# GpSimd issues none of the last output tiles' stores, with another order of the work

## The chip, the cores and the metric

The kernel runs on one core of one Trainium2 chip. The core has a matrix engine (TensorE, PE in the profile, with its weight loads as PEld), VectorE (DVE), ScalarE (ACT), GpSimd (POOL) and SyncE (SP), which run side by side and wait for each other on semaphores. Transfers between device memory and on-chip memory are DMAs; in this kernel SP, ACT and GpSimd issue them. The metric is the time of one execution on the device in microseconds (us). 13 runs of the kernel before gave a median of 248.54 us, from 246.45 to 251.24.

## The reference

Attention through 32 packed queries per head, and then a feed-forward layer with a squared ReLU:

```python
def _attn_ref(q, k, v, p):            # q, k, v: (8, 8, 576, 64), p: (8, 8, 32, 64)
    p_packed = sm_attn(p, k, v)       # softmax(p k^T / 8) v
    out = sm_attn(q, p_packed, p_packed)
    ...
x = attn_out.transpose(0, 2, 1, 3).reshape(4608, 512)
h = x @ w_in                          # (512, 2048)
r = np.maximum(h, 0.0)
out = (r * r) @ w_out                 # (2048, 512)
```

## The kernel before

The work is cut by batch (8 batches of 576 tokens) for the attention and the first matrix product, and by output tiles of 128 tokens (36 tiles, 0 to 35) for the second product. The kernel doesn't issue its work in the order of the source. It builds steps, each a chain of pieces, and every piece has one or more alternatives: an engine, an estimate in us and a function that issues the instructions. `Plan.run` (L62) then issues all 1,696 pieces in an order written out by hand in the string `ORDER` (L77): decoded, it is one 16-bit number for each piece, in which the low 12 bits are the place in the order and the upper 4 choose the alternative, so the engine. Every engine runs its own instructions strictly in the order in which they were issued; waits between engines follow from the data and the buffers. The estimates in the code have no part in the order once the string is there.

The names of the steps that the text uses, with batch b, tile t:

- `Lk.b.q`, `Lq.b.q`, `Lv.b.0.i` (L661 to L677): loads of k, q and v, issued on GpSimd, which casts float32 to bfloat16 on the way. v comes in four parts (i = 0 to 3). `LWI`, `LWO`: the two weights. Eight buffers hold k and q, two hold v.
- `Cv.b.q` (L686): a copy of v into one tile, `v_b` (L251), on DVE. It needs all four parts of v, and the buffer of v is free for batch b + 2 after it.
- `Tk`, `Tq` (L691): transposes of k and q on DVE, and for batches 4 to 7 of q as DMA transposes on SP (L281).
- `S1`, `PV`, `XT`, `M`, `S2`, `N`: the attention, with q's side folded into w_in by `M`. `X.b` on GpSimd lays out p. `XT.b` takes the packed result out of PSUM (`pp`, `pq`, `rD`), and `S2.b` needs that.
- `R.b.fb` (L790): four matmuls of the first product for one of 16 blocks of 128 columns, and the ReLU out of PSUM on ACT (L499) or DVE (L501), through two PSUM tiles `ps_h`. `F1.b.fb` (L798): the square of two such blocks into `gT`, mostly on DVE (L510). Four buffers `r` lie between, each of two blocks.
- `F2.t.fb` (L850): the second product for one tile. Tiles 7 to 34 are done in groups of four (L896) with seven half-size products instead of eight, `F2.t.n.kk` with n = 1 to 7; `WS.t.n.h` (L882) are the sums of g that they need, on DVE (L606). Results leave the PSUM banks `ps_o` on ACT (L170) or DVE (L172, L633) into one of three output buffers `o_sb`. The last tile, 35, is done in two halves of 256 columns (L861), the first evicted by DVE, the second by ACT.
- `ST...` (L827): the stores of an output tile, in pieces of two DMAs of 32 rows each (64 KB; 32 KB for a half of tile 35). Each piece may go to SP; to GpSimd from tile 8 on, and to ACT from tile 31 on. A group's tiles t and t + 1 are stored after its product 6 (`ST.t.6`), t + 2 and t + 3 after product 7 (`ST.t.7`).

`FILL` (L75) names steps in front of whose matmuls TensorE runs extra ones on a tile of zeros (`keep_clock`, L190), 97 in all, in the first 27 us.

In the order before, the last 24 DMAs of the stores (tiles 31 to 35) are 10 on GpSimd, 6 on SP and 8 on ACT.

Of the kernel before, what the change touches and what calls it, by code (L numbers as in the profile page):

```python
# [76 lines left out]
ORDER = (  # L77
    'c-jrt17j5m7y!`EVd3s-)mm;DtJSit)t23smR2phwrsm)+qP}nw)x(#I0rx=2_%A~kP{3NLssyC<d6rFfg6H>At7V}FQkRy;0t~b0;wS*l!E+F'
    '0IESQ2!cvb1}Z``C<$dD9I8Vd=mQO)IgEx*&<z$sD`*chpfc2iE>Ig9!VstcRiQ16fU$5G2E$0$3QZsqCPGgb0IOjEEQM>Z9M-`tm;jUEEKGyh'
    'a0xcUPIv@2;2tEvy>JNLzzH}9-{B5C1t&g+*N_HZzz4{Tf<9OQ^I#$DitpeH1fv^MV_p0Tf1wzb#!A==t6(i0h&8c3j>kaEjV*C8uEmp>5wl@q'  # L80
    'oPi5)54ORMxEkl<ay)=f@eL9+$F?{ZH{x!*hVStQ`cX~_p_cRtKcX*9!CAN&SK<~thei%6Lf`NYrls_hjj9n-BFamXXcn!cxwM!zQYy+smFW>a'
    '!w)!?rqB|q%}sd#XQ3c!K-IY}_vQf3#QC`ix8k8ZgXYsZy2RJ{F_+=0+?p$KICtjJG=XMPDo)2a_zK_Q_gsieazif0<+wR#<Gfs%GjdKY$_NS$'
    'AV>iIkPb39(mMhn3uJQ?0w=h@11F&<6oXgr9!B6;{EEM^EA^*j?B=PwjO$5PNdYM#4Wx1eIL<>NOo=-%DV?QBoEdUJFSr6Vurpr5JNOS%6R`3k'
    'KE;(KO7cQ^Xbdet(Tg*2116*jRFSGuZ>mXkr~_@GU38ST(>}UD-}oOVl0S@+N|K6O0>vd>36kuP8}dOBC<uk21eAtyPzA!Eh9eYi!hN_4Pv9B6'
    'gpcqUe!?#YVKM~Y_Sgmc-~{ZCgK#>o!cDl<_Yj`K`@RqG2|mZq_zr&|l2Bqw?krB_ojGU~ZK5@Fg7(r8I!EW}GF_otbc3EyPwvb8c@z)gaXgu)'
    '@C=^C3wXY39%qvrl1qw9J}DxlrL2^f3hpqeDOKG^<+vP^Q*v5v%L92VPvyD$wY-xz?pjb6>N)zsFo=aUupTx#w!jY9?O=3ZDh$PT*Z?2n3*VQR'
    'm5Nb5I!>pYr|BBqcHW^rJdlU*7@o+}IlJVS+)_+RNg4MEIVYFpt~_)<l6KlzJ9_%)AkP4;4^5#FL_lk32OXg$w1E!L8KNK>x<U+ehe0qLdO&aJ'
    '4{?wIb72+?!6H}<Yhz(7i(%LVe<F~QliZYn3Xq5VDLa*<<+PgC(^lF+7wH3Sqy6-VUeQZ>L!ame{U+vm{F9JVZ~<P*>v#ok;qAPikMTC%!$<fQ'
    '*OB_tR9Z?K=_iAwqjZ*$vQ$cH8Lg^~w5hh&?%F~lHA?$xUl`~Z3ZoojV7y}-OoAye(=i?9z<gK?OJD_ThkbAmj=~W*1!v$gT!5=^9UeL!z*~3@'
    'pB&w=H}=53z5{SL4#8144yWNnoQLta6qn&TT#vhOJMPDWcoYxgaXgLZ@d94PD|j7m;BBlzH7JzAsV+69Ce*?iNm0~}qNxjYqwds)`q3a7OmWU('  # L90
    'G=fIbIGRY)XgbZId9;8Q(o!N$$O$+JCuJ9VIHfB!r{@fug|l-I=i`E0m`ibKuE15e7Kd?tZp@L~lB2jCcjQhS!~6K4>oA|-lYEBH@&&%kH~1z$'
    ';79y|U-BD%$DjEN|Kh)_Vv<;rh_5)sPy8jVJB_55*3w?ONH^&ry`_)zcMp^y5-Y=Ggp6~Kmx(e}X38v?C-Y^IES6=mLRQNfSua~;hwPNS@>V{$'
    '-^&;Gcljm1<)5&ciYC@1np_>~Qjezc_-lZs(~O#3b7@`;)&g2s!?mu~)&@F4N9!mZ>zSaFb&^iknL0=3>T+GCt9703)-Af%b4<_a1-<OKsyFnO'
    '-qrj1NFVD{eW9;BQz0H!!8W)Ex8Vnv?_ivSD{vnk!LxW1A7UeFPd#ZMjiRZvh*nTq4&*#sf@^RKj^<u`o}ch5{>mZ_$tYQ+mrRx!GFKMLI@u#f'
    'B$4{6pC_~C)M8pro9jHC@7d%zqSy6~KG%;r4;H~nSPQ#g5A25n@DCDVI!uq5FgxbOd{_Wy!CY7d8(<S0gX3@-{s3Z8EQL|n38OIv`{6hE4T&)c'
    'CdK6Fi!StFR?LC<u?$wkde{&n&<|6fKL%i0%!%c&Dptoj*a(|qGi-s8*c!WI5EjJZSRPwp2kePnil?=-fi}}_I!Mpx8+GS?JeXs71W(|Nyp>Z*'
    'PRT35Qb=k`b7>{p<fNRD3vyNN$q)G>q^e0ZpBB{WI$THURGp;@b*XOEQ~FcE5}VunExl#6oL1e!Z6uDtIk*tF;a)t3C-4kj#H)A<@8Ugtjc+lt'
    '^Amo-@AwxJkPjuHWaOe0l#&7{4W*-u6iBt4c_=>xQ$Z?BMX3apqS92B%26e%PGMA=8d7s=MiJDCI#Oqfp<dLNVrc*kp`kRK#?W}0OtWbj?W8?)'
    'fDX}NIz}hy3|*&7bd_$>UAjm2=>a{Y7xb8((sO!EZ|NPqr;qfDKGPTaO5f=Z{iS~-oS2Ohu@5`h%l@2(Gjn-YR?f}A9Kyx9ELY@e+}2fx8*npj'
    '!yUK_cjF#Bmg9IB59g6Qn#c1rp2>@OHqYU?9M21R2`}fByxO&j*YH|i&l`9XZ{{7mi+A#F-pdF05Fh2^e44NFIljo(_%=V}r~I1V@(0%^{>i_Y'  # L100
    'C8798GVw@iNg)A}PBKU)$t+nUkCc!CQcyyquoRV&QcfyL4XGqmq?%NhP^l&1Qdb(e8%RTGEKQ`Dw2%milupuC+DQkAmKf<SJ*BS<l>stH;$*mt'
    'k_j?Nrpqe#Y>AfzvP724N?9u#<dAHY-Lg;i%K<qoXXU)yl#6mnuE;gHE;r<s+>!h8M4rhDc`2{tqkNLj@=d<VPx&kVqpt}xq57y-lc`hPnnF`*'
    'YE7eQHN9rgOd6;;G`Hs05G|smJVmv*meA5#R?BN;t)jKGn%2-z4bysBUmI#;ZKcgLLR)HUZKG|qgLcxM8m(QltHx+I?V-K2xAxQiI#37e5RKJ1'
    '9je20qK?sVI$o#fG@YTdHC|Wh0$rqwb&0OfRk}vk>SoV2-KBeUpYGR#dRUL@2|c4{^}JrxD|$_D>TP|X_w=DY(P#QnU+WuvtMB!le$Y?)S-<F4'
    '{ifgbm;TV-`bYojKm9+0#-=7_mcSBPBJ;5%mei74GIN-(In8ArOKGVrz*1WpOJ^A@qXk+v%Wk<Whvl{)%V+s5*a})9D`JJMs1>skR?<pYX)9yp'
    'tgMx{3Rcl7S!JtYRjr0qvrwyPwJgkPTOF%w^{t*Yu!h#i8e0=<YR#;LHMa<hw3gP&T3dVTV4ba_b+TydVlmdux?2zHX}zqU^|t{w$Oc=i4YxQO'
    'Y9nl<jk3`;#>U$On`o14icPg?Hr-~}EGvN}u`-5ZERM!uI2Ge?GS0>&I20G*8r+GwC^r?NGE|S6QhjPmt*H%lq8^l-9qh-sT)wU%9LhDhy{i#N'
    'xVrLPe(t)*&-lLUBY$TQa{q88kmNF2#<-`sr^r~DBO7It>~e3H&F+JeMYC!)Pmm{%7Sak@QEPfCdFptY=z86t+jXPofS%MHdfIcyv(s~2FR9lG'
    'n4hJ!6yD;N$+B1;%k0hT4Y4-XHn6KV%G!B{Sa0iN1HF9%hXqcyu{O>-(>u>*+Z>x47;papcrZuK'
)  # L110
# [918 lines left out]
```

## Time and profile before

| what | value |
|---|---|
| median of 13 runs | 248.54 us (246.45 to 251.24) |
| the profiled execution: its time, its span | 249.91 us, 248.0 us |
| mean granted clock of TensorE | 0.981 of full speed |
| GpSimd: store DMAs x58, mean of one | 28.7 us, 502 ns |
| ReLU on ACT (L499) x97, on DVE (L501) x15, mean of one | 650 ns, 755 ns |
| square on DVE (L510) x60, mean of one | 752 ns |
| 64 KB stores, median from issue to landing: SP, GpSimd, ACT | 2.8, 2.3, 3.5 us |
| chain that ended last, share of PE / DMA / DVE / POOL | 69% / 13% / 6% / 3% |

The page gives times of one profiled execution; it took 1.37 us more than the median of the runs, and its span, from the first to the last instruction, is 1.9 us shorter than its time. In the rows by slices the span is cut in 40 equal parts of 6.2 us, and a digit is the busy share in tenths. PEclk is the clock that TensorE was granted. A wait names the engine and line that waited, what released it, the total, how often and the longest.

### The profile page before, as it was taken

How to read it: one execution, taken by the hardware profiler on the slowest of the kernel's cores; microseconds unless marked ns; L12 is line 12 of the kernel's file. 1: busy time of each engine (PE TensorE's matmuls, PEld its weight loads, DVE VectorE, ACT ScalarE, POOL GpSimd, SP SyncE). 2: the span in 40 equal slices, each digit the busy share in tenths (PEclk: the TensorE clock that was granted, in tenths of full speed). 3: DMA queues.
4: the chain of work that ended last, by engine and by line, in shares of the span. 5: the costliest groups of instructions: out<-in, count | busy, mean ns of one | idle time of the engine just before them, and what ended most of it. 6: DMA issues, size and time to landing. Idle time of an engine off the chain costs nothing.

```text
span 248.0 us, 6006 instructions
## 1 busy us (share of the span) xinstructions
PE 227.6 (92%) x2407; PEld 174.1 (70%) x2417; DVE 180.9 (73%) x315; ACT 158.8 (64%) x265; POOL 88.8 (36%) x177
## 2 busy tenths in 40 slices
PE   8587989999999889999969999999999999999960
PEld 6465556467656756888648878887888788888850
DVE  3666779689997588988768699798887698765400
ACT  3337468799978759788848776878576857412110
POOL 8585468517573012083711400141007005104070
PEclk9799999999999999999999999999999999999995
DMA  6999999999999995079950980032005104206070
GB/s 215 180 206 203 198 200 207 204 228 213 232 204 216 169 188 95 3 130 179 228 95 15 158 189 3 6 102 68 1 3 146 27 0 108 65 3 169 0 213 1
DMA packets 35708, 31.43 MB, mean 127 GB/s; under 512 B 15232, under 2 KB 28160, under 8 KB 35680
## 3 DMA queue, kind: packets, MB, share of 16 engines
q0 software_dynamic: 21328, 21.67, 51.3%
q1 hardware_dynamic: 13824, 8.33, 15.3%
q10 hardware_dynamic: 528, 1.05, 1.3%
q8 instruction: 19, 0.31, 0.5%
q14 instruction: 9, 0.07, 0.1%
HBM read 37.22 MB, written 9.44 MB: 188 GB/s over the span
## 4 chain that ended last, share of the span: by engine, by line
PE 69%; DMA 13%; DVE 6%; POOL 3%; ACT 2%; issue 2%; POOLq 0%; SPq 0%; DVEq 0%
PE ps_o L620 30%; PE ps_h L470 17%; DMA k_b<-in_k_dram 4%; PE ps_o L561 4%; DMA q_b<-in_q_dram 3%; PE ps_h L480 3%; DMA v_r<-in_v_dram 3%; PE ps_m L383 3%; DMA k_f<-in_k_dram 3%; PE ps_a L561 3%; PE ps_a L296 2%; PE ps_pp L331 2%; PE ps_s L192 1%; PE ps_s L444 1%; POOL out_dram L541 1%
## 5 line engine op out<-in xcount | busy, mean ns | idle before, releaser
L499 ACT ACTIVATE r<-ps_h 128x576 bf16<-128x576 f32 x97 | 62.5, 650 | 21.4 <-PE ps_h L470 18.8
L470 PE MATMUL ps_h<-a,M 128*128 128x288 bf16 x448 | 71.7, 286 | 1.7 <-DVE r L501 1.5
L541 POOL DMA_DIRECT2D out_dram<-o_sb x58 | 28.7, 502 | 101.9 <-DVE o_sb L633 91.9
L510 DVE TENSOR_TENSOR gT<-r 128x1152 bf16<-128x1152 bf16 x60 | 44.8, 752 | 13.4 <-ACT r L499 10.1
L470 PEld LDWEIGHTS <-M 128*128 128x128 bf16 x448 | 43.7, 98 | 12.5 <-issue 2.1
L620 PEld LDWEIGHTS <-wS 128*128 128x128 bf16 x448 | 42.6, 98 | 9.3 <-issue 3.2
L620 PE MATMUL ps_o<-wT,wS 128*128 128x256 bf16 x336 | 41.7, 273 | 0.4 <-DVE wS L606 0.4
L620 PEld LDWEIGHTS <-gT 128*128 128x128 bf16 x336 | 32.7, 98 | 5.7 <-issue 0.2
L620 PE MATMUL ps_o<-w_out_b,gT 128*128 128x256 bf16 x224 | 32.5, 273 | 0.0
L170 ACT COPY o_sb<-ps_o 128x512 f32<-128x512 f32 (+1 forms) x24 | 13.8, 575 | 24.4 <-PE ps_o L620 21.1
L247 POOL DMA_DIRECT2D v_r<-in_v_dram x32 | 19.3, 609 | 24.3 <-DVE r L501 9.4
L170 ACT CAST M<-ps_m 128x1024 bf16<-128x1024 f32 (+1 forms) x26 | 23.5, 930 | 2.7 <-PE ps_m L383 2.5
L561 PE MATMUL ps_o<-w_out_b,gT 128*128 128x512 bf16 x72 | 21.2, 380 | 0.5
L606 DVE TENSOR_TENSOR wS<-gT 128x1024 bf16<-128x1024 bf16 (+1 forms) x32 | 19.1, 617 | 0.2
L633 DVE TENSOR_TENSOR o_sb<-ps_o,o_sb 128x512 f32<-128x512 f32 x21 | 14.4, 684 | 5.1 <-issue 2.9
L561 PEld LDWEIGHTS <-gT 128*128 128x128 bf16 x112 | 10.1, 98 | 10.3 <-issue 2.0
L620 PE MATMUL ps_o<-wT,gT 128*128 128x256 bf16 x112 | 16.3, 273 | 0.0
L620 PE MATMUL ps_o<-w_out_b,wS 128*128 128x256 bf16 x112 | 15.8, 273 | 0.0
L501 DVE TENSOR_SCALAR r<-ps_h 128x576 bf16<-128x576 f32 x15 | 11.2, 755 | 5.9 <-PE ps_h L470 5.9
L192 PEld LDWEIGHTS <-idle_b 128*128 128x128 bf16 x97 | 11.1, 118 | 6.3 <-issue 3.8
L458 DVE SCALAR_TENSOR_TENSOR a<-e,rD,ls 128x576 bf16<-128x576 bf16 (+1 forms) x18 | 13.0, 743 | 2.8 <-ACT ls L452 2.7
L438 ACT ACTIVATE e<-ps_s,rD 128x576 bf16<-128x576 f32 (+1 forms) x18 | 11.4, 683 | 4.8 <-PE ps_s L430 2.8
(84 smaller groups left out, 317.8 us busy)
## 6 DMA issues: line engine op xcount, KB each, us to landing
out_dram<-o_sb SPq DMA_DIRECT2D x80, 64.0 KB, 2.8
k_b<-in_k_dram POOLq DMA_DIRECT2D x14, 288.0 KB, 9.6
q_b<-in_q_dram POOLq DMA_DIRECT2D x14, 288.0 KB, 8.4
out_dram<-o_sb POOLq DMA_DIRECT2D x54, 64.0 KB, 2.3
v_r<-in_v_dram POOLq DMA_DIRECT2D x16, 160.0 KB, 7.8
v_r<-in_v_dram POOLq DMA_DIRECT2D x16, 128.0 KB, 8.4
w_in_b<-in_moe_w_in_dram POOLq DMA_DIRECT2D x8, 256.0 KB, 9.2
w_out_b<-in_moe_w_out_dram POOLq DMA_DIRECT2D x8, 256.0 KB, 9.0
```

The costliest lines, as they stand in the source:

```text
L170: nc.scalar.copy(dst, src)
L192: nc.tensor.matmul(ps, lhsT=idle_b[:, :P], rhs=idle_b, start=True, stop=True)
L247: nc.gpsimd.dma_start(self.vr[32 * i:32 * i + 32, h0:h1, :n * D], src[:, :, J0[i] * D:(J0[i] + n) * D])
L458: nc.vector.scalar_tensor_tensor(out=self.a2[:, qd, n0:n1].rearrange("p (c n) -> p c n", n=HALF), in0=self.e2[qd, hf], scalar=self.rD[:, q ...
L470: nc.tensor.matmul(ps[:, c, :HALF], lhsT=a.M[:, qd, fb * FB:(fb + 1) * FB], rhs=a.a2[:, qd, c * HALF:(c + 1) * HALF], start=(qd == 0), sto ...
L499: nc.scalar.activation(dst, src, ACT.Relu)
L510: eng.tensor_tensor(out=dst, in0=r, in1=r, op=ALU.mult)
L541: eng.dma_start(dst, src[32 * i:32 * i + 32])
L561: nc.tensor.matmul(po[t], lhsT=gT[:, fb, n0:n0 + P], rhs=w_out_b[:, fb, :], start=(fb == 0), stop=(fb == NFB - 1))
L606: eng.tensor_tensor(out=dst, in0=a, in1=b, op=op)
L620: nc.tensor.matmul(ps[:, u * EH:(u + 1) * EH], lhsT=lhs, rhs=rhs, start=(n in (1, 2, 4) and kk == 0 and u == 0), stop=(kk == KB - 1 and u ...
L633: eng.tensor_tensor(out=o, in0=ps, in1=o, op=ALU.add)
```

## The change

One condition in `store_step` and the two tables change. No arithmetic is changed, and no buffer.

```diff
-FILL = {'S1.0.0': 31, 'S1.0.1': 4, 'PV.0.0': 12, 'M.0.0': 16, 'N.0.0.0': 11, 'S2.0.1': 3, 'N.0.0.1': 10, 'R.0.0': 1, 'R.0.2': 3, 'R.0.1': 4, 'R.0.4': 2}
+FILL = {'S1.0.0': 30, 'S1.0.1': 11, 'PV.0.0': 14, 'M.0.0': 9, 'N.0.0.0': 6, 'S2.0.1': 2, 'N.0.0.1': 9, 'R.0.0': 1, 'R.0.2': 3, 'R.0.1': 4, 'R.0.4': 1}
 ORDER = (
-    'c-jrt17j5m7y!`EVd3s-)mm;DtJSit)t23smR2phwrsm)+qP}nw)x(#I0rx=2_%A~kP{3NLssyC<d6rFfg6H>At7V}FQkRy;0t~b0;wS*l!E+F'
+    'c-jTQ17H;Z6ac{I)zaTr=4z|8Y-3rAtJbn@yQSq?Timj3+qP}n?hZg8G5A4pC;$e&5C{n&3FLsJ;DmfYkN{FcB1i_g!2{`_D5L>@C<{fP1k{88'
...
                         for e, us, eng in (("SP", 0.86, nc.sync), ("POOL", 1.0, Q), ("ACT", 0.86, A))
-                        if e == "SP" or t >= (8 if e == "POOL" else 31)]
+                        if e == "SP" or (8 <= t < 31 if e == "POOL" else t >= 27)]
```

What the new order says, decoded from the two strings:

- Stores. GpSimd may store tiles 8 to 30 and ACT tiles 27 to 35. Of the 74 store pieces GpSimd has 18 (29 before), SP 48 (41) and ACT 8 (4). Of tiles 31 to 35, SP and ACT have 12 DMAs each. GpSimd's last pieces are one of tile 28 and one of tile 30.
- 62 pieces run on another engine: 23 stores, and 39 on ACT or DVE (11 ReLUs, 10 evictions of `F2`, 6 of `M`, 5 of `XT`, 5 squares, 2 casts in the head). Of the squares, `F1.7.15` and two others go to ACT and two to DVE.
- In GpSimd's queue the loads of batches 2 to 7 stand in another order. Among them: `Lv.4.0.1` has 0.9 MB more (of float32 read) ahead of it; `Lv.6.0.1`, `Lv.6.0.2` and `Lv.6.0.3` stand ahead of the first stores of tile 7's group, and `Lv.6.0.0` is the seventh load behind them.
- On DVE, `F1.2.5` and `F1.2.7` stand ahead of `Cv.4`, and `R.2.9` goes to ACT. On TensorE, the `R.2` blocks come up to five pieces earlier among the products of tiles 6 and 7, `R.7.13` to `R.7.15` up to 15 pieces later; most others move by one or two places.
- On SP the eight transposes remain, and `Tq.6` and `Tq.7` come ahead of the stores of tiles 11 to 14.
- On ACT, in the end, the eviction of tile 35's second half stands behind ACT's stores of its first half.

More of the change, by code (lines that the diff above doesn't have):

```diff
@@ L72, in run @@
             fn()
-FILL = {'S1.0.0': 31, 'S1.0.1': 4, 'PV.0.0': 12, 'M.0.0': 16, 'N.0.0.0': 11, 'S2.0.1': 3, 'N.0.0.1': 10, 'R.0.0': 1, 'R.0.2': 3, 'R.0.1': 4, 'R.0.4': 2}
+FILL = {'S1.0.0': 30, 'S1.0.1': 11, 'PV.0.0': 14, 'M.0.0': 9, 'N.0.0.0': 6, 'S2.0.1': 2, 'N.0.0.1': 9, 'R.0.0': 1, 'R.0.2': 3, 'R.0.1': 4, 'R.0.4': 1}
 ORDER = (
-    'c-jrt17j5m7y!`EVd3s-)mm;DtJSit)t23smR2phwrsm)+qP}nw)x(#I0rx=2_%A~kP{3NLssyC<d6rFfg6H>At7V}FQkRy;0t~b0;wS*l!E+F'
[L79 to L109, printed above, removed]
@@ new lines @@
+    'c-jTQ17H;Z6ac{I)zaTr=4z|8Y-3rAtJbn@yQSq?Timj3+qP}n?hZg8G5A4pC;$e&5C{n&3FLsJ;DmfYkN{FcB1i_g!2{`_D5L>@C<{fP1k{88'
+    '$OcuQIFyEZ5CWB;15}1uFc8{8XP65WpgQz|ZqOGNLv09$QBWV6zyv4-<)Jx@gUN6NB4Ir2fCy*_(_sJ%gSD^_R={<b3NdgNX2N{9469)i+<|Sd'
+    '7aqY)cmRU?;4r*}Q*aT!!aaBjPJ9fnAw4EUKP-T0&>!n#VJwS-kkJ=&;6G3d#AKKPD`6JQj%_dmtKe|VjYY8s*2Zw0j193F&OtAx!<x7PH{$_p'
+    'j_q+FcEvup9Pi;H{Dd2D2Oh_5xDPKOQxZx`l_-?@(m_0l&u}rW#+|qu58*A$PbH`>6{QerLdhv36(S%dC;5__ve7(RMq9{1sVFy{!1MSD(^C*t'
+    'p<vF>mAMR6r4AIr)wmB&p&7K0VkwSR(gd1HbEzVS@*oc299*1RaR;8nvuFXWq3T?ZM{r$^;4z$+i*OkGb2cu(CAd6y<bqs^n=pcc0~mZD6QqX>'
@@ new lines @@
+    'j*Jil*&*1G2VCHGc;PgZgfj37-oZGWg5U5Lj-=6KoQ~)7Ms6TIB?Y8}%#g~F)^Q15!e^L)S?MyxaTdr0J>eQO!CrU`AEF=mQ&LXO*Z3CKm9CN('
+    '3PEFN0f-))h3oJSmZu6-od!`G>O|vcC+(+Gw1*DUH5$v4c@|ILX}p5>^D#chhxsJm;jEAo@<U-L2*scrRD`Nf4eCM-2zA_s`*0VYz%zIO@8J`C'
+    'gYS+%kOa-IGj_*;I2DKD2%L$_a6NAHJB(-Xso!&ajc@P^e!!pj50Q)#I~!1CX93zs+i5eMq@#3>uFzGwNw?@V-J=IIn1^vB&*V`&o#S~PFXAP<'
+    'lGnIabC3i}PAMUIrKpsV5GgMe+*KshUDbV5j>|DQCFkX~JdkJdLSDK*$s6})sRIq5p<@t?hT*UVHo#WLcGv~G9fT<{G1kJ4*a%<ZTfcW0NX01+'
+    'ouvzO(Rqg+J0H?e9?4N0%X4`lXP11EONvWbcWF5x=j5{7m51&}(m^|Wy6FHN<{6@4&<L7BGiU|vp%b)*Hqa5eLObXJ-Ju8chM_P9`anMz3?m>j'
@@ new lines @@
+    '=EAI41WRCbtcS(1Jl4Us_yhkUQBrbICJLrxl#;SjNm@%AXe;fay>y+v(QZ0IFX#ikryul*{t<B^ZqC3yoPkU82Hwe=`2Zi`^ZbC1@@c-pFS(9{'
+    'Nn>d#ZDf!Pmrl|}qGW-T)M{EzBeaQj)ZW@$TWWh9sQqDxV<e1)D3}BjVG2xx8ID+(4f9|TEP!RO2M)kNI10z$1e}C(a2~F}Rk#5U;SD^856~M2'
+    'U_Tt}Hw>e2Bu>Cd7>m;}4(H(_T!O1`EpEpxxEJ^1F+75&@f=>pD|j7m;BCBv53m~5q#9J)S)U@P5jAzTq_)(Wx=>f@MZIYN4WuD7lp<*qjio4>'
+    'M3X6+rqgViLyKrJEvJN>jFYgJQ*ati%Nbo+IEb@zZqCO=xfqw>a$JS0axJdIjkrEH<Cffx+jD2`#=Ts<xj&!fi>}LjgKzR(zQ+&wF+bzy{EFZ3'
+    'd;Y-R_y_;tzf2;MND_-foZ^+_l2X!2Mt27BmsZkVx=SzVBmHH740aEd5fUk*WvoncPnM|?BeP_-#LIkHB#UL4tdP~RMmEV7*&(}Rue_4C?sxJ*'
@@ new lines @@
+    'e#me6DgT62)ij|dRfi^1r^l<QJSjDeX4K4@MYC%z&8zvekk-}u8m8eoR>$i&o#>gW(=}RW>Ku*J`MO9~=_cK#yLE>i^qkWRdS0*Sb-k&#^`5@g'
+    'xB5mu=uiEl(GUkKVI5q6TksKnJ0dX#m*O5giWl)NzQ9)0jr!0q8c#8_gw|13&c%hf5;x$sJdlU*6aL6QStW^hB#UH|eiAJ+B~F&gTG=f}#7Etp'
+    '<Qk;8wT9NwW*Va_Jv;S?=bApyPs-kSSOTkHJ#2)Xa2(FS7x)VqFcSt~Hq3+huprKYIj|I#!)Dk5`{5A$fS*tdD`PwCfZebs4#8gl=z|F`5hg_k'
+    'y3mb57>xO`43@(N7=f)YIi|wYm=-f)PON~{um*-<V{D2ouqC#}PS_XoVj(Pv6)_aMV1G<V@wADy(GEI5$LJ0Hq3%4KNAozI$}@NmALKNWL-I&|'
+    'DJj*ZxwMw8a#GI71-U8r<eU5wP*#5}pry2ej?rm4TNmnTU8h_1xc*WwHMjX&u;sOaR^95@c$|iFaRF|^U3d!5;03&jH}O6`#wYk5KVoX<XZ(ua'
@@ new lines @@
+    '@iz+jPy$Ls9`aHON<--=17)ThRF85|Udl%WsW26zQdFACQaP$fwWtn-QDbUG9i1(xJ$0s@)Q<+!2pU7HX(COdnKYl4(h6Ed>*);bql0vaj?)P`'
+    'P3P$n-K86Jo9@#idO}a>89k?W^palDTlz?!=?i_O?}Yr5e$j9GOU%N`3D}ntvy0vA;nbX-GjSl-bmincT!>3@S+2k}xHk9T#@v)!b0_Y?J-Htb'
+    ';5j^=C-M}I<`|yM3wSZFb1mg%yqs6@T3*kacnfcHZRPE}gLm<6-pl*=5Fh6ge2UNT1-`^r`8wa`w|t);@l$@mulXH+;_nRZUyQ=yE6K!9+>%1l'
+    'Nh(P%nIy9WNT6hu+)`KyNI@wiMWmRNl5$c}YDp!jEY+lj)Rfv%PwGpAyP<?jBWWT{rJ1ylw$ee`Nk{1{-K2-~mcBAjM#&HvCL?8xjFTxcO=ieS'
+    '_Z*og3uTEcmsPS(Hp?N|CVOO`?3V*_SWe4Xxhfasl3bB%a$Ro7Ex9B2<*_`Gr}A80%X|4KU*x-dl|S-VP(>4{uO`wYnppkRr5;V8sWq*p(+rwk'
@@ new lines @@
+    'Gif#r)*PBg3u<94>M5edwS<Ofd9A3Gw2Ic!>KdvwwYE0UhT2FQYin()Ewq)k(YD%7J82i~t6jCb_RyZ%OZ#X)?XQD$unyJXIzl6Lq>j?j8l@9-'
+    'l1|ns8mlvOmd@3A8m|j<u`bsYx>ncg2Hmb3b&KxN1A0gg>rp+SXFMnMl%Cd0dRedP4ZWpz^se65hx$k#>l1yd&-8^p*O&TA-|2h(sGs$Ve)oLU'
+    'Z~8-j>tFq+Xk-aZ%*@9Un6D+W#FoU8SyFSDpE=EC9!q7ZEv+|=rLzo{(K1<}WwY#-({flY%VYU0zZI}TR>X=~Q7djGtfZB)(pJXGS~+ismA493'
+    '(JEPGt728HhE=mrt7)~Yw$-(I7G@2szBROPYh)4D*qT^VYi`Y~g|)O+*4o-w2kU5Eyq&DGb+sPW(|TEN>tlVbpAE3VHq?gMa2sKxEYe2WSc|f8'
+    'Hr^)KB%5qgEZU}9tj(~QHp^yPDJ+duu`Z6nvA7bq;%J<R(HM_oa6Zn)HJF8RQUDd9h7?ZCsU3Bv{?vnplY{*@C8u&ZU75KdhjSZO3-0Rb%b)q5'
@@ L110 @@
+    '>kEH%{bmy%Nh%543B@I;WxPy~Sod_9=$<R<WrOT=Z<mekgA$;Dn$?qEb80ayt(CQmR`rzi)YB!pMwfav>oVP?d-bgD(_^~db5XsP-jZ7iZ_0om'
+    '%WPRKw`K7L1QfQm*3P<l+k3m)5bJLPZL|&Yj`7CWM4M{UymM@>#aX;}p8W?I$45>'
 )
```

## The prediction

> **What bounds the kernel now.** I read the page's engine and slice rows first, then the gaps of TensorE, then what ends last. TensorE is busy for 227.6 of 248.0 us, so three places are left: the head, two holes in the middle, and the end after the last matmul.
>
> ```profile
> PE 227.6 (92%) x2407; PEld 174.1 (70%) x2417; DVE 180.9 (73%) x315; ACT 158.8 (64%) x265; POOL 88.8 (36%) x177
> ...
> PE   8587989999999889999969999999999999999960
> ```
>
> The second row's 6 in the 21st slice and the last digit are a hole and the end. The end, by stretches (columns: PE, PEld, DVE, ACT, POOL busy, granted clock), and the instructions of the program's last line:
>
> ```profile
> 235.00:240.20 5.20, 4.65 (x43) 3.91 (x40) 0.56 (x2) 0.95 (x2) 4.48 (x10) 1.00 0.67 185
> 240.20:248.00 7.80, 0.00 (x0) 0.00 (x0) 0.00 (x0) 0.01 (x1) 0.41 (x1) 0.61 0.17 47
> ...
> L1024 POOLq DRAIN x3: 46/102/7180, 240.0 to 247.7; - x3
> L1024 SPq DRAIN x3: 7/7/7, 243.4 to 247.5; - x3
> ```
>
> Nothing computes from 240.2 on. The last store lands at 243.05, SP has seen every landing at 243.4, yet GpSimd's closing drain runs from 240.04 for 7.18 us, to 247.22; the other engines' last steps wait for it, and 0.75 us later the span ends. The end is GpSimd's drain, 3.8 us behind the data.
>
> The holes, as waits in 76 to 95 us (first two lines) and 110 to 130 us (last two):
>
> ```profile
> DVE v_b L172 <- DMA k_b<-in_k_dram: 2.9, 1, 2.9
> PE ps_h L470 <- DVE r L501: 1.5, 1, 1.5
> ...
> DVE v_b L172 <- DMA v_r<-in_v_dram: 3.5, 1, 3.5
> PE ps_s L413 <- DVE pp L172: 2.0, 1, 2.0
> ```
>
> Twice VectorE stands at a cast of v (Cv) whose last load is late; the work queued behind it, an eviction of PSUM (L501) and the extraction of pp, is what TensorE misses: gaps 85.98 to 87.45 and 124.77 to 126.79. From 127 to 239.6 TensorE has no gap, so what is saved before reaches the end. In the second hole the chain of waits reads:
>
> ```profile
> 118.47 7.25 DMA v_r<-in_v_dram
> ...
> 125.91 0.49 DVE v_b L172
> 126.40 0.34 DVE pp L172
> 126.79 0.29 PE ps_s L413
> ```
>
> **The end.** Of the 24 store DMAs of tiles 31 to 35, before has 10 on GpSimd, 6 on SP, 8 on ACT; after has 12 and 12 on SP and ACT. GpSimd's last DMAs become those of tiles 28 and 30, due about 223 to 226 us. It then drains: 226 + 7.2 = 233, beside matmuls that run to 239.6. If that cover failed, the drain would cost its 3.8 us again.
>
> What is late next is the last landing. The trace gives each DMA its semaphore: SP and ACT share eight, GpSimd has eight others, and a store waits until the previous one on its semaphore has landed (ACT's store at 238.87 follows a landing at 238.85). Before, 14 stores share SP's and ACT's eight; after, 24, in four rounds:
> - tiles 31, 32: ready 235.16 as now, eight issues to 236.4. Their first landing stays at 238.67 (a 16 KB instruction fetch sits on one DMA engine from 236.19 for 1.37 us); landings then come 0.18 us apart, to 239.9.
> - tiles 33, 34: their eviction goes from ACT (0.58) to DVE (0.69), done at 236.9. They need those semaphores: issues from 238.7, four per queue at 0.42, to 240.3; landing about 2.0 later, 240.7 to 242.3.
> - tile 35, left: issues 240.7 to 241.4. One pair is on ACT ahead of the last eviction (L170, 0.37), which moves from 239.84 to about 241.9.
> - tile 35, right: issues 242.3 and 242.7, landing 2.2 later at 244.9.
>
> SP's waits take 0.4 and the close 0.75: 246.05 against 248.0, **-1.95**. Bounds: with no semaphore waits the last landing stays at 243.05 and the end is 243.43 + 0.75 = 244.2, -3.8; with 0.4 more in each of three rounds, -0.75. Here the Trainium skill (DMA: Bandwidth & Descriptors, "Issuing engines are not separate DMA queues") says that all issuers run on the same 16 DMA engines and several issuers save only the issuing time. By that rule the third queue is given up for nothing and the sum is -3.8; the row of ACT's store at 238.87 shows a wait that it leaves out. I take the row.
>
> **First hole.** The loads are moved in GpSimd's queue. From 30 to 88 us landings follow bytes in order, about 0.35 MB (as float32 read) per us. The last load for Cv.4 (Lv.4.0.1) had 27.4 MB up to it and landed at 84.5; after, 28.3 MB, and 28.3 MB had landed at 86.5. So it comes 2 us later. But VectorE's queue is changed to match: two squares (F1.2.5, F1.2.7) now stand ahead of Cv.4, and the eviction R.2.9, which held TensorE, goes to ACT. With those two squares done, the four r buffers hold all the rest of batch 2, and TensorE need not stop. What it needs next is F2.7.3, behind WS.7.2 on VectorE: from the landing, two casts (1.0), four squares (0.75 each) and three sums (0.68) = 6.04, so 86.5 + 6.04 = 92.5 against 94.14 now: **-1.6**. TensorE without gaps would reach it at 92.05 (gaps 1.46, 0.40, 0.23), so at best -2.1; landing at 88.1 gives 0, and each us more costs one; I bound it at +1.5 (its place in the queue gives an issue near 77; with the 10.5 us that this load now takes to land, 87.5, and 2 more for a longer backlog, 89.6).
>
> **Second hole.** Before, the last load for Cv.6 was the eleventh load behind the store that waits at 106.27. After, three of its four loads go ahead of that store, and the last (Lv.6.0.0) is the seventh behind it: 3.1 MB instead of 4.6. Before, 3.1 MB of these had landed by 122.1; I allow 1 us, as both pairs of tile 7's GpSimd stores now stand in front: 123.1. The matmul follows its landing by 1.1 (125.7 to 126.8), so it is ready at 124.2 and TensorE comes at 124.7: the gap goes, **-1.9** (0 to -2.4 with the 0.43 before it).
>
> **Head.** Filler matmuls: 97 to 90 (S1.0.1 4 to 11, M.0.0 16 to 9, N.0.0.0 11 to 6, PV.0.0 12 to 14, four others one less). The granted clock by its own windows, TensorE alone:
>
> ```profile
> 6.45:9.86 3.41, 1.36 (x16) 1.00 1.36 196
> 9.86:13.28 3.42, 2.93 (x21) 0.50 1.18 170
> 13.28:16.69 3.41, 3.41 (x75) 1.00 1.22 201
> 16.69:20.10 3.41, 1.97 (x32) 1.00 1.18 208
> 20.10:23.52 3.42, 2.90 (x43) 1.00 1.23 204
> ```
>
> A window with 1.36 busy was followed by half clock; one with 1.97 was not. Seven fills more in the first (0.097 each) make 2.04: half clock should go, and 12 fills of 167 ns become 97, -0.84. Five fewer in the fourth leave 1.48, near 1.36: it may cost half of the next window's 2.90, +1.45. The skill (TensorE: Matmul & The Clock Gate, "What's actually happening") takes the clock away only after a window of about 3.4 us without work; by it both edits leave the clock alone and the shorter chain gives -0.5. The row contradicts it, so I keep both ends. The gain is also capped: PV.1.0 at 38.8 stands on Cv.1, whose last load lands at 37.3 at the same place in the queue; with R.0.14 off VectorE, Cv.1 can start 0.6 sooner. Sum **-0.3** (+1.5 to -0.6).
>
> **The rest.** 62 pieces change engine, evictions and squares between ACT and DVE mostly. From 95 to 160 us TensorE's order hardly changes; later, R.7.13 to R.7.15 move back by up to 15 pieces, but WS.31 still has 37 products of 0.218 = 8 us for about 6 us of work. Where TensorE is full, moves cost nothing unless they make a gap. The small gaps after 37 us that I named no cause for (0.25, 0.40, 0.23, 0.43) are the nearest row: new ones of that size, **+0.5** (0 to +2.5). On SP the eight transposes stay, but the last four now go ahead of tiles 11 to 14's stores: the third rival.
>
> **Sum:** -1.95 - 1.6 - 1.9 - 0.3 + 0.5 = -5.25, in the profiled execution 249.91 to 244.7. That execution is 1.4 above the median of the 13 runs; on the median, 248.54 - 5.25 = 243.3.
>
> **Rivals.**
> 1. *The holes only move.* As many bytes come before as ever, and Cv.4's last load is later, which speaks for it; that work was put in front of both casts, and that Cv.6's loads come early, against. Then the tail alone: 248.5 - 1.95 = 246.6.
> 2. *The drain does not go.* The few words say the last eight tiles; GpSimd still stores half of tiles 28 and 30. That is 14 us before the end, so the cover holds. But the drain may follow the last landing of any queue: now it ends 4.2 after 243.05. For it: the drain before any DMA took 0.19. Against: nothing in it waits on SP or ACT. Then 244.9 + 4.2 + 0.75 = 249.85 in the span, +1.85; with -3.3 elsewhere, 247.1.
> 3. *SP becomes the bound, slower.* Its last four transposes took 7.3 us of issue (136.85 to 138.47, to 141.66, 143.79 to 146.51). Now they stand ahead of group 11's stores. If their q loads and the free qT let them start by 127.7, they end by 135.0, when those stores are due, and cost nothing (Lq.6.0 landed at 127.8 and is now four loads earlier). From then on each us late holds an output buffer of three, then an eviction, then a bank of ps_o; starting at 136.85 as now, all 7.3 show: 243.3 + 7.3 = 250.6.
>
> **Chances.** Forecast 0.58, its own range 240.6 to 245.5 (all gains at their best, -8.9, are unlikely together; -7.9 is taken); rival 1 0.22, rival 2 0.09, rival 3 0.11. The range 240.6 to 247.6 takes in rivals 1 and most of 2. A measurement of this kernel tells about 0.5% (1.2 us) from no change: faster gets the forecast, 0.20 of rival 1 and 0.04 of rival 2, 0.82; the same 0.06; slower 0.12.
>
> **What would show it.** The end: POOL's drain beginning before 230 and over by 235; SP's drain setting the end, 5 to 7 us after the last matmul; ACT's last eviction behind its stores. Holes: no TensorE gap over 0.5 near 86 and 125; Cv.4 at about 86.5 and F2.7.3 at 92.5; Cv.6 near 123 less what was saved before. Head: full clock near 10 us and kept at 20. It is wrong if TensorE's idle time between 37 us and its last matmul does not fall by some 3 us, or if the drain ends last again.

## The result, and the profile after

The kernel after takes 242.94 us (median of 11 runs, 241.85 to 246.9) against 248.39 (48 runs, 246.45 to 253.09): a ratio of 0.9796, with a 95% interval from 0.9764 to 0.9828, or 5.1 us less (4.3 to 5.9). Its profiled execution has a span of 241.9 us (243.62 in time), before 248.0. Runs more than 1.5% above the fastest run of the same kernel are left out of this ratio and of those below.

The rows by engine and by slices, of the kernel after:

```profile
PE 225.8 (93%) x2400; PEld 172.7 (71%) x2410; DVE 178.9 (74%) x310; ACT 161.5 (67%) x270; POOL 78.6 (33%) x155
...
PE   7688989999999997999899999999999999999990
```

The 6 of the 21st slice is gone; what is left of the holes is the 7 of the 16th (90.7 to 96.7 us). The last slice is still empty. By stretches the end is now (PE, PEld, DVE, ACT, POOL busy, clock), with the instructions of the program's last line below:

```profile
235.00:238.43 3.43, 1.19 (x11) 0.82 (x9) 0.00 (x0) 0.37 (x1) 0.00 (x0) 1.00 0.74 192
238.43:241.85 3.42, 0.00 (x0) 0.00 (x0) 0.00 (x0) 0.00 (x0) 0.00 (x0) 0.70 0.14 39
```

```profile
L1024 POOLq DRAIN  x3: 46/102/5185, 222.2 to 241.6; - x3
L1024 SPq DRAIN  x3: 7/7/13, 241.0 to 241.3; - x3
```

GpSimd's long drain begins at 222.2 and takes 5.19 us, beside matmuls that run to 236.2. The last store lands at 240.56, SP closes at 241.0, and that is the end. The waits in 76 to 95 us (first two lines) and in 110 to 130 (the last):

```profile
DVE v_b L172 <- DMA v_r<-in_v_dram: 3.4, 1, 3.4
...
PE ps_o L620 <- DVE wS L606: 1.6, 1, 1.6
...
PE ps_o L620 <- DVE wS L606: 0.6, 1, 0.6
```

VectorE still stands at Cv.4, until 87.3, and TensorE still stops for it, but later and at other work: no longer at an eviction (L501), but at the sums of F2.7.3, from 91.37 to 92.98. At Cv.6 nobody waits any more.

Where the 6.16 us between the two spans arose, read off the first weight load of the same pieces in both traces:

| up to | before | after | difference so far |
|---|---|---|---|
| R.0.0 | 22.30 | 20.94 | -1.36 |
| PV.1.0 | 38.79 | 37.60 | -1.19 |
| R.2.0 | 76.73 | 76.16 | -0.57 |
| F2.7.3.0 (behind hole 1) | 94.14 | 92.98 | -1.16 |
| S2.5 (hole 2 in front) | 126.79 | 123.65 | -3.14 |
| end of the last matmul | 239.65 | 236.19 | -3.46 |
| end of the span | 248.01 | 241.85 | -6.16 |

Some 2.0 us came at the second hole, 0.3 between it and the last matmul, where TensorE has no gap over 0.05 us in either trace (the cause of these 0.3 is open), and 2.7 behind the last matmul. The head and the first hole together gave 1.2.

### The profile page after: what moved, and what is told of

Same layout as the page of the kernel before. It is cut to its first block, busy times and chain, and to the rows that moved or that the text cites. A ratio compares the mean times of both kernels' runs of the same rounds, so it can differ in the third digit from the quotient of the medians.

```text
span 241.9 us, 5995 instructions
## 1 busy us (share of the span) xinstructions
PE 225.8 (93%) x2400; PEld 172.7 (71%) x2410; DVE 178.9 (74%) x310; ACT 161.5 (67%) x270; POOL 78.6 (33%) x155
## 4 chain that ended last, share of the span: by engine, by line
PE 65%; DMA 19%; DVE 5%; POOL 4%; issue 2%; ACT 2%; SPq 1%; DVEq 0%; ACTq 0%
PE ps_o L620 34%; PE ps_h L470 19%; DMA v_r<-in_v_dram 5%; DMA out_dram<-o_sb 4%; DMA p_b<-in_p_dram 4%; DMA w_out_b<-in_moe_w_out_dram 4%; PE ps_m L383 3%; DMA p_f<-in_p_dram 2%; PE ps_a L296 2%; PE ps_pp L331 2%; DVE gT L510 1%; DVE wS L606 1%; PE ps_o L561 1%; POOL pT_bd L172 1%; SPq L541 1%
## 5 line engine op out<-in xcount | busy, mean ns | idle before, releaser
L470 PE MATMUL ps_h<-a,M 128*128 128x288 bf16 x448 | 70.9, 286 | 0.6 <-ACT r L499 0.4
L510 DVE TENSOR_TENSOR gT<-r 128x1152 bf16<-128x1152 bf16 x59 | 43.5, 753 | 13.2 <-ACT r L499 9.2
L541 POOL DMA_DIRECT2D out_dram<-o_sb x36 | 17.9, 502 | 99.2 <-DVE o_sb L633 86.5
L170 ACT COPY o_sb<-ps_o 128x512 f32<-128x512 f32 (+1 forms) x20 | 11.5, 573 | 22.4 <-DMA out_dram<-o_sb 10.8
L501 DVE TENSOR_SCALAR r<-ps_h 128x576 bf16<-128x576 f32 x14 | 10.6, 756 | 6.4 <-PE ps_h L470 6.4
L172 DVE COPY o_sb<-ps_o 128x512 f32<-128x512 f32 (+1 forms) x15 | 10.0, 669 | 5.3 <-PE ps_o L620 4.1
## 6 DMA issues: line engine op xcount, KB each, us to landing
v_r<-in_v_dram POOLq DMA_DIRECT2D x16, 128.0 KB, 6.5
```

The source lines that it names most:

```text
L170: nc.scalar.copy(dst, src)
L172: eng.tensor_copy(dst, src)
L470: nc.tensor.matmul(ps[:, c, :HALF], lhsT=a.M[:, qd, fb * FB:(fb + 1) * FB], rhs=a.a2[:, qd, c * HALF:(c + 1) * HALF], start=(qd == 0), sto ...
L510: eng.tensor_tensor(out=dst, in0=r, in1=r, op=ALU.mult)
```

## Experiments

Each kernel below was measured beside runs of the kernel before on the same chip, and is given as a ratio to them. The level of those runs moved between three sets of kernels (medians 249.5, 249.8 and 248.8), so ratios are compared, or kernels of one set. All have one addition to `Plan.run`, which lets a table give a piece another place or engine (in three kernels, where only fillers change, the table is empty):

```diff
-        for c, p in sorted(zip(code, pieces), key=lambda x: x[0] % 4096):
-            e, us, fn = p.alts[c // 4096]
+        for c, p in sorted(zip(code, pieces), key=lambda x: edit(x[1])[0] or x[0] % 4096):
+            e, us, fn = next(a for a in p.alts if a[0] == edit(p)[1]) if edit(p)[1] else p.alts[c // 4096]
```

An entry reads (step, stage, number): (place, engine). Where a kernel made from after stores a tile above 30 on GpSimd, that alternative is added back.

### The end alone, and the end undone

The kernel before, with its ten last GpSimd stores on SP and ACT:

```diff
+    ('ST.31.6', 1, 1): (None, 'ACT'),
+    ('ST.31.6', 1, 3): (None, 'SP'),
+    ('ST.31.7', 1, 1): (None, 'SP'),
+    ('ST.35.0', 1, 0): (None, 'SP'),
+    ('ST.35.0', 1, 1): (None, 'ACT'),
```

> The kernel before with one thing changed: the five pieces of GpSimd's stores of tiles 31 to 35 (ten DMAs) go to SP and ACT; order, fills and loads stay. Theory (GpSimd's closing drain set the end, and stores issued earlier on GpSimd drain beside matmuls): about -2.7 us, what the tail from the last matmul to the end lost between before and after; TensorE reaches its last matmul when it did before. Rival (the new order gave the gain): 0. Rival (the drain follows the last landing, whoever issued it): +1.9.

Measured: 0.9827 (0.9771 to 0.9883), 4.3 us less (2.9 to 5.7), where 2.7 was expected. In its trace the last matmul ends at 239.86, as before; from there to the end are 5.07 us instead of 8.36, so -3.3. The last line of the program:

```profile
L1035 POOLq DRAIN  x3: 46/98/6467, 226.3 to 244.6; - x3
L1035 SPq DRAIN  x3: 7/7/13, 244.1 to 244.4; - x3
```

The drain is done at 232.8, and SP sets the end. The order has no part in this gain, and the drain does not follow the landings of other queues: the last of them is at 243.88, 11 us after it.

The kernel after, with the same five pieces back on GpSimd (each entry 'POOL'):

> The kernel after with those same five pieces given back to GpSimd; its order stays. Theory: the drain of some 7 us at the end is back, +2.7 us against after, which is -3.4 against before; what is left is the gain ahead of the last matmul. Rival (the new order set the end): as after, -6. Rival (drain follows the last landing): a little faster than after, since fewer stores wait for SP's and ACT's semaphores.

Measured: 0.9844 (0.9786 to 0.9902). Its tail is 7.37 us against 5.66, +1.7, so a us less than expected. By the ratios it stands 1.2 us above after, and the two intervals overlap, so the cause is read from the trace. The drain:

```profile
L1036 POOLq DRAIN  x3: 46/102/6303, 235.7 to 242.5; - x3
```

It ends at 242.03, 3.3 us after the last landing of all stores, and sets the end again. It is 0.9 us shorter than before's 7.18; I had taken that for fixed.

### How long the drain is, and where it may begin

Two kernels made from after. In the first, one piece of tile 35's right half (two DMAs) goes to GpSimd; in the second, two pieces of tile 31 (four DMAs):

```diff
+    ('ST.35.1', 1, 0): (None, 'POOL'),
```

> The kernel after with one piece of tile 35's right half (two DMAs of 24) on GpSimd, issued at about 238.5. Theory (GpSimd's drain starts when its queue ends and costs about 5 us from its last issue, however few DMAs it has to close): drain from about 238.9 to 244 or later, +3 to +5 us against after. Rival (the drain's length goes with the DMAs since the last one, 7.2 us for ten and 5.2 for four): about 4.5 us, +2. Rival (the drain costs nothing beyond the landing): 0.

```diff
+    ('ST.31.6', 1, 1): (None, 'POOL'),
+    ('ST.31.6', 1, 3): (None, 'POOL'),
```

> The kernel after with two pieces of tile 31 (four DMAs, issued at about 232) on GpSimd; the last stores stay on SP and ACT. Theory (only where the drain starts matters, and SP's and ACT's stores wait for their eight shared semaphores): the drain ends by 239, beside the other stores, and four fewer stores wait for semaphores: 0 to -0.8 us against after. Rival (any GpSimd store of the last tiles costs a drain at the end): +1 or more.

Measured: 0.9889 (0.9822 to 0.9957) and 0.9792 (0.9722 to 0.9863), after being at 0.9796. By the ratios the first is 2.3 us slower than after: below the 3 to 5 of its theory, near the 2 of the rival in which the drain's length goes with the DMAs; the interval holds both. The two kernels stand in one set, and the first is 2.1 us slower in the median than the second. The drain in the first and in the second:

```profile
L1032 POOLq DRAIN  x3: 46/102/5545, 238.0 to 244.1; - x3
```

```profile
L1033 POOLq DRAIN  x3: 46/102/6402, 232.1 to 240.2; - x3
```

Two late DMAs bring a tail of 9.28 us, 3.6 more than after, though the last data land at 239.79, earlier than in after. Four DMAs at 231 to 233 cost nothing: their drain ends at 238.5, while the last store lands at 239.46; the tail is 5.46, 0.2 shorter. So what counts first is when GpSimd issues its last DMA: two late ones cost 3.6 us, four earlier ones nothing. In the 14 profiles the drain ends 4.8 to 6.6 us after the end of that issue, and never less than 2.42 us after the landing of GpSimd's last DMA. Between these values the number of DMAs does go along with the length: with two or four in GpSimd's last 15 us the drain ends 4.8 to 5.5 us after the issue, with six to ten 5.6 to 5.8, with twelve 6.6. Whether the number is the cause is not shown. Four stores fewer on SP and ACT shortened the tail by only 0.2 us; the stores that were left still waited for semaphores (one starts at 235.55, after a landing at 235.49), so this does not measure what all the waits cost.

### Hole 2: the load of v tile 6

The kernel before, with three loads moved in GpSimd's queue:

```diff
+    ('Lv.6.0.1', 0, 0): (664.5, None),
+    ('Lv.6.0.2', 0, 0): (664.7, None),
+    ('Lv.6.0.0', 0, 0): (822, None),
```

> The kernel before with three loads of v tile 6 moved in GpSimd's queue, and nothing else: two of them to behind the first, ahead of the store that waits at 106, and the last one to ahead of the last loads of tile 7. Theory (the hole at 124.8 to 126.8 is that load's lateness, and TensorE has no gap behind it that would swallow the gain): the gap of 2.0 us goes, -2.0 (with the 0.4 ahead of it -2.3). Rival (holes only move to another load, here tile 7's): 0 to -0.5.

Measured: 0.9879 (0.9838 to 0.9921), 3.0 us less (2.0 to 4.0). The windows over the old hole:

```profile
119.07:122.48 3.41, 3.30 (x63) 2.51 (x64) 3.38 (x7) 3.08 (x5) 3.05 (x6) 1.00 0.68 159
122.48:125.90 3.42, 3.42 (x46) 2.69 (x44) 2.73 (x8) 2.77 (x5) 0.00 (x0) 1.00 0.86 129
```

TensorE is busy throughout; the last matmul ends at 236.37 (-3.3), and the tail is before's 8.36. Of these 3.3 us, 0.86 arose ahead of F2.7.3 (Cv.4 runs at 83.64, not 84.50) and 2.09 between F2.7.3 and S2.5, which is the hole. Three loads do what the whole new order does at this place, and no other hole opens: the rival falls.

### Hole 1: what stands behind the cast, or the load

The kernel before, with the casts behind the two squares and R.2.9 on ACT:

```diff
+    ('Cv.4.0', 0, 0): (639.4, None),
+    ('Cv.4.1', 0, 0): (639.6, None),
+    ('R.2.9', 1, 0): (None, 'ACT'),
```

> The kernel before with the two casts of v tile 4 put behind the squares F1.2.5 and F1.2.7 in VectorE's queue, and the eviction R.2.9 on ACT; the load stays where it was, so it lands at 84.5 as before. Theory (the hole at 86 to 87.5 comes from what is queued behind the waiting cast, not from the load itself): the gap goes, -1.5 to -2.1 at the end, more than the change itself kept of it (0.6), because the load is not 2.8 us later here. Rival (the work behind the cast is only late elsewhere): 0 to -0.6.

Measured: 0.9984 (0.9934 to 1.0035), no change that the runs can tell. In the trace the gap at 86 is indeed gone, and R.3.0 comes at 102.58 instead of 104.27, -1.69. It is lost again at the second hole. The windows of this kernel there, then those of the kernel before:

```profile
122.37:125.78 3.41, 1.28 (x23) 0.62 (x20) 1.42 (x5) 0.60 (x2) 0.70 (x2) 1.00 0.86 148
125.78:129.19 3.41, 3.41 (x31) 2.34 (x17) 2.87 (x6) 1.62 (x3) 0.00 (x0) 0.50 0.15 21
```

```profile
122.48:125.90 3.42, 2.29 (x37) 1.85 (x32) 0.00 (x0) 1.38 (x2) 2.12 (x6) 1.00 0.89 168
125.90:129.30 3.40, 2.47 (x33) 1.86 (x34) 3.33 (x9) 2.20 (x4) 0.00 (x0) 1.00 0.69 114
```

In both the hole is 2.0 to 2.1 us long. In before it lies across the border of two windows of the clock, and both stay at full clock. Here it lies within one, that window is left with 1.28 us of work, and the next runs at half clock: full work in 3.41 us at half clock is worth 1.71, just what had been won. The last matmul ends at 239.66, as before. So the theory on what held TensorE is right, and the gain did not reach the end in this execution; for the runs together it is not shown.

The kernel made from the tail alone, above, shows the same at its hole, 122.74 to 125.71: 0.73 us of work, then half clock. It had reached F2.7.3 2.0 us sooner than the kernel before, and nothing of that is left at its last matmul.

```profile
122.01:125.42 3.41, 0.73 (x7) 0.41 (x5) 0.59 (x2) 0.00 (x0) 1.54 (x4) 1.00 0.61 103
125.42:128.83 3.41, 3.12 (x27) 1.82 (x28) 2.92 (x8) 2.25 (x4) 0.00 (x0) 0.50 0.46 70
```

Now the load itself. The kernel after, with one load moved ahead of five others, the first of them one of k tile 5:

```diff
+    ('Lv.4.0.1', 0, 0): (534.5, None),
```

> The kernel after with one load moved: the last of v tile 4 goes ahead of a load of k tile 5 in GpSimd's queue. Theory (the gap at 91.4 to 93.0 is the landing of that load at 87.3 and the 5.7 us of VectorE work from it): the load lands some 2 us earlier, the gap goes, -1.2 to -1.7 us against after (-7.4 against before). Rival (the k load that is now behind it is the next to be late, or VectorE is late for other reasons): 0.

Measured: 0.9695 (0.9647 to 0.9742), 7.6 us less than before (6.4 to 8.8), where after stands at 5.1. The load lands at 76.6, 10.7 us earlier than in after and not some 2. VectorE no longer waits for it: Cv.4 runs at 82.8 instead of 87.3, and the window in which F2.7.3 now comes shows no hole:

```profile
88.90:92.30 3.40, 3.38 (x51) 2.48 (x48) 3.39 (x6) 3.35 (x7) 0.79 (x3) 1.00 1.23 191
```

The remaining hole was that load. The gain over after, 2.5 us by the ratios, is more than the 1.2 to 1.7 expected; the next section shows a cost of the hole beyond its length. The six runs of this kernel lie between 240.78 and 241.72, those of before beside them between 246.3 and 251.84.

### The fillers

The kernel after with before's `FILL`, and then the kernel with the early load, with the same edit:

```diff
-FILL = {'S1.0.0': 30, 'S1.0.1': 11, 'PV.0.0': 14, 'M.0.0': 9, 'N.0.0.0': 6, 'S2.0.1': 2, 'N.0.0.1': 9, 'R.0.0': 1, 'R.0.2': 3, 'R.0.1': 4, 'R.0.4': 1}
+FILL = {'S1.0.0': 31, 'S1.0.1': 4, 'PV.0.0': 12, 'M.0.0': 16, 'N.0.0.0': 11, 'S2.0.1': 3, 'N.0.0.1': 10, 'R.0.0': 1, 'R.0.2': 3, 'R.0.1': 4, 'R.0.4': 2}
```

> The kernel after with the filler matmuls of before (97 instead of 90); order and queues stay. Theory (what the head gained, 1.0 us at the first matmuls of row group 1, is swallowed where TensorE waits for a load that lands when the bytes ahead of it have landed, at 87.3): 0 within 0.3 us at the end, though TensorE is later by up to 1.2 us at 40 us. Rival (the head's gain reaches the end): +0.6 to +1.2 against after.

Measured: 0.9724 (0.9653 to 0.9796), the ratio of the three lower runs. The six runs fall in two groups, 241.65 to 242.65 and 246.65 to 247.96, three in each, so on the fillers this comparison decides nothing. The profiled execution (247.88) is of the slower group, and its trace shows what the first hole can cost. TensorE comes to it at 90.40, a us sooner than in after, whose head had a window at half clock. The load comes no sooner: Cv.4 runs at 87.93. So the hole is 3.2 us long instead of 1.61, one window is left with 1.24 us of work, and the next two run at half clock:

```profile
89.15:92.56 3.41, 1.24 (x15) 0.71 (x12) 3.34 (x6) 2.85 (x6) 2.00 (x4) 1.00 1.00 176
92.56:95.97 3.41, 2.37 (x14) 1.81 (x15) 3.39 (x6) 0.38 (x1) 1.14 (x4) 0.50 1.31 152
95.97:99.38 3.41, 3.41 (x43) 1.86 (x42) 1.22 (x1) 1.56 (x3) 0.86 (x3) 0.50 1.27 181
```

F2.7.3 is 0.6 us later than in after, the last matmul 3.2 us (239.43). Coming sooner to a wait for a load can thus cost time. That the other two runs of this group, and those of after above 245, have the same cause is likely and not shown, as they have no trace.

The same edit where no hole is left:

> The kernel after with that load moved and, besides, the filler matmuls of before (97 instead of 90). There is no late load left between 36 and 115 us that could swallow a delay of the head, and the runs of its neighbour without the old fillers spread by 0.9 us only. Theory (the new fillers made the head 0.6 to 0.8 us shorter, read at R.2.0 over the profiles of both kinds): +0.6 to +0.8 against the neighbour, 242.0 to 242.2. Rival (the fillers do nothing for the end): 241.3 to 241.5.

Measured: 0.9709 (0.9669 to 0.975), median 241.73 of five runs, 0.4 above its neighbour of another set: between the two theories. The trace is clearer. R.0.0 comes at 20.56 instead of 19.11, so the old fillers do cost 1.4 us in the head; but the first weight load of PV.1.0 comes at 36.88 against 37.02, and the last matmul ends at 233.33 against 233.41. The waits in 28 to 40 us, first with the new fillers, then with the old:

```profile
DVE v_b L179 <- DMA v_r<-in_v_dram: 1.4, 1, 1.4
```

```profile
DVE v_b L179 <- DMA v_r<-in_v_dram: 0.4, 1, 0.4
```

VectorE stands at Cv.1 until its load has landed, to 36.5 and to 36.3, and PV.1.0 needs Cv.1. What the head wins is waited away there. In these two executions nothing of it is left at the last matmul; the 0.4 between the medians has no counterpart in front of it, but lies behind: the tails are 6.15 and 6.62 us.

### Fillers in the holes

The kernel before with sixteen fillers ahead of S2.5 (and, in `s2_x`, a call of `keep_clock` for the first tile); the kernel after with fourteen ahead of N.3.0:

```diff
+'S2.5.None': 16
...
+                    if qd == 0:
+                        keep_clock(ps[:, 0, :224])
```

> The kernel before with sixteen filler matmuls (1.5 us) ahead of S2.5, where TensorE stands for 2 to 3 us at 125; nothing else is changed. Theory (a hole costs more than its length where it falls in one window of the clock: windows of 3.41 us with 1.38 us busy or less were followed by one at half clock, windows with 2.29 or more were not): no half-clock window behind the hole in any execution, so the runs of this kernel spread less than those of before (246.3 to 253.7 in the two calls so far), none over 250, the median 0.5 to 1.2 below before. Rival (the spread comes from the loads alone): spread and median as before, or +0.5 where the fillers hold TensorE up.

```diff
+'N.3.0.None': 14
```

> The kernel after with fourteen filler matmuls (1.3 us) ahead of N.3.0, two matmuls before the hole at 91.4; they run just ahead of the hole, and what comes behind it waits for VectorE as before. Theory (4 of the 11 runs of after stood above 245 because the hole fell in one window of the clock and the next ran at half): median 242.3 to 243, and no run above 244.5. Rival (the spread comes from the loads): a third of the runs above 245 as in after.

Measured: 0.997 (0.9943 to 0.9998) and 0.9739 (0.9693 to 0.9785). The windows of the first over hole 2, and of the second over hole 1:

```profile
123.23:126.65 3.42, 3.30 (x44) 2.66 (x42) 1.34 (x5) 0.88 (x3) 1.22 (x3) 1.00 0.78 131
126.65:130.06 3.41, 3.41 (x45) 2.86 (x31) 3.15 (x7) 2.50 (x5) 0.00 (x0) 1.00 0.38 56
```

```profile
91.01:94.43 3.42, 1.80 (x19) 1.32 (x16) 3.39 (x6) 2.06 (x4) 2.05 (x5) 1.00 1.34 194
```

Neither execution has half clock behind the hole. The first kernel gains 0.7 us, within what was expected, but one of its 12 runs stood at 251.37, against the forecast that none would pass 250, and before itself had only one of 17 over 250 in this set: on the spread this run decides nothing. The second has its median at 242.39 and its highest run at 243.93, as expected; with 4 of 11 runs above 245 in after, six runs without one come by chance about once in 15 times, so this speaks for the theory and doesn't prove it. Its trace adds nothing here: the trace of after has no half clock behind this hole either.

### Load and eviction: the fastest version

The kernel with the early load, and one pair of tile 35's left stores behind ScalarE's last eviction:

```diff
+    ('Lv.4.0.1', 0, 0): (534.5, None),
+    ('ST.35.0', 1, 1): (1690.5, None),
```

> The kernel after with the load of v tile 4 moved as in the last call (which ran at 0.9695 of before) and one piece of tile 35's left stores put behind ScalarE's last eviction. Theory (that eviction starts about 2 us after TensorE's last matmul, because a pair of stores that waits for semaphores stands ahead of it on ScalarE): the eviction starts within 0.5 us of the last matmul, tile 35's right half is issued 1.5 us earlier, and the tail from the last matmul to the end goes from 6.15 us to 4.7 to 5.4: 240.0 to 240.7 us. Rival (the eight shared semaphores bind either way, since 24 DMAs must land in the same order): tail as it was, 241.3.

Measured: 0.9675 (0.9635 to 0.9715), median 240.88 of six runs (240.77 to 241.31): faster than before by 8.1 us (7.1 to 9.1), and below after. That it is faster than the early load alone (241.36, in another set) is not shown by the times, and the median is above the 240.0 to 240.7 expected. The tail is 5.63 us against 6.15, where 4.7 to 5.4 were expected. ScalarE's evictions at the end:

```profile
L178 ACT COPY o_sb<-ps_o x2: 372/479/586, 225.1 to 235.2; 128x512 f32<-128x512 f32 x1, 128x256 f32<-128x256 f32 x1
```

The last starts 1.4 us behind the last matmul (233.82) and not 0.5: ScalarE's stores of tiles 33 and 34, which wait for semaphores until 234.4, stand in front of it too. To move these as well was not tried.

## Why the prediction was right

Forecast were 243.3 us and a sum of -5.25; measured are 242.94, and -5.1 by the ratio, -6.16 by the two profiled executions. Where the gain would come from was right: the end, the second hole, and a part at the first. That the sum is so close is in part luck: the first hole gave less than forecast, and the end, the head and the rest more. One of the prediction's own signs of being wrong did occur: TensorE's idle time between 37 us and its last matmul was to fall by some 3 us and fell by 1.9, from 5.2 (197.42 us busy of 202.65) to 3.3 (195.84 of 199.19), because the first hole moved and did not go. The terms, one by one:

**The end, -1.95, was -2.7.** The mechanism held: the drain begins at 222.2, it is hidden, SP's drain sets the end, the second and third of four rounds of stores wait for landings (SP's second store of tile 33 starts at 235.29, just after the landing at 235.27), and the last eviction stands behind stores. The fourth round does not wait for semaphores: it starts at 238.45, when that eviction is done, and its semaphores had been free since 238.32 or earlier. Two terms were too large. The last eviction starts 1.9 us after the last matmul, not 2.25 (241.9 less 239.65); and for the time from issue to landing I took 2.0 to 2.2 us from stores of before, while tile 35's took 1.5 to 1.9, its last 1.7. The rule of the skill that I weighed here would have given -3.8, so the truth lies between rule and row.

**The first hole, -1.6, was -0.6 of its own.** The load landed at 87.3 and not at 86.5; what follows took 5.7 us and not 6.04. But a second step was wrong in form: the head's -0.3 and this term were added, although F2.7.3 follows the landing, whatever was won before. In after, in the tail undone, in both kernels with other GpSimd stores and in the one with fillers in the hole, F2.7.3 comes 5.68 us behind the start of Cv.4, to the hundredth, and 5.67 in after with the old fillers. Head and hole together were forecast at -1.9 and gave -1.16. That the load is 2.8 us later than before was the price of the new order here, and the early load shows it: with that load earlier the same order is 2.5 us faster by the ratios.

**The second hole, -1.9, was -2.0:** Cv.6 ran at 121.5, and the gap is gone. The loads alone do it.

**The head, -0.3, was -1.36 at R.0.0 and -0.57 at R.2.0,** for other reasons than mine. The half-clock window was to go; it came in the profiled execution of after too, at 7.67. The clock that I feared to lose at 20 us was not lost. Both questions hang on where the grid of windows falls, which differs from execution to execution: in the profiles of after and before one window of the head is at half clock, in two of the other twelve as well, in ten not. What shortened the head is the filler chain itself, for which I had 0.5 us: two kernels that differ in the fillers alone, neither with half clock in the head, stand 1.45 us apart at R.0.0 (19.11 and 20.56). The cap at Cv.1 was right, and the run with the old fillers shows it. Of the 0.6 us lost again between PV.1.0 and R.2.0, 0.39 is one new gap at 55.4.

**The rest, +0.5, was about -0.3:** no gap over 0.05 us arose between S2.5 and the last matmul, and that stretch is 0.3 us shorter than before. The new small gaps that I had feared are the one at 55.4 and 0.65 instead of 0.43 at 118.4; they are counted in the terms above.

Of the rivals, "the holes only move" is half true for the first hole, which went from 86 to 91 us, and false for the second. "The drain does not go" falls by the kernel with the tail alone, and SP's transposes were through at 128.0, before the stores that they stand ahead of.

## What to carry to other kernels

Look at what each engine does after its last useful instruction: a queue whose last DMA comes late can end the kernel without any data moving, and it is enough to let that queue finish early. Ahead of a gap, follow one load to the work that waits, and count a gain in front of it only as far as that wait allows; here moving one load was worth half as much as the whole change. A gap that is long against the clock's window can cost more than it shows (1.3 to 2.6 us more in three of these traces), in some executions and not in others, so judge such kernels by many runs and by their windows, not by one profile.

## What the runs showed of the hardware

- GpSimd's closing drain took 5.1 to 7.3 us in the 14 profiles, with two to twelve DMAs in its last 15 us, and it was longest (7.2 to 7.3) in the four with twelve; SP's and ACT's took 0.01 and 0.15.
- The clock window. Put on the grid of 3.41 us that each profile shows, and from its first record of the clock on, every one of the 13 windows with some matmuls but at most 1.43 us of them was followed by half clock, holes and tails alike, and of the windows at full clock with 1.47 us or more a single one (2.04, in the head of before with fillers in hole 2), which I can't explain. So work in about 43% of the window (1.47 of 3.41) was enough but for that one, and a single gap costs clock only from about 2.0 us on (3.41 less 1.43). The skill (TensorE: Matmul & The Clock Gate, "What's actually happening") names an idle window of about 3.4 us as the condition; if that means a window without any work, the runs contradict it. The hole of after, 1.61 us, is too short by that; the one of 3.2 us in after with the old fillers was not.
- Kernels without a gap of 2 us spread little: 0.9, 0.5, 0.5 and 1.3 us from lowest to highest (five or six runs each: the three with v tile 4's load early, and before with v tile 6's), against 5.5 to 7.1 for before beside them. That the clock makes the difference is likely from the point above, but the run with fillers in hole 2 did not settle it: late loads vary too (Cv.4 ran at 86.2 to 87.9 in the profiles with after's order).
